# Later weight slices begin at stepped offsets inside longer buffers, in an attention and MLP kernel

## The chip, the cores and the metric

The kernel runs on one core of a Trainium2 chip. The metric is device time in microseconds (us) for one execution. A core has five engines that take part: TensorE (PE, with its weight loads shown apart as PEld), VectorE (DVE), ScalarE (ACT), GpSimd (POOL) and SyncE (SP), which issues transfers. Operands lie in an on-chip memory of 128 partitions; an address below is a byte offset within a partition.

## What is computed

Attention over 2 x 8 heads of 768 tokens with head size 64, masked so that a query sees only keys of its own hash bucket; then an MLP in two parts over the 1536 tokens. The weights named w1 to w4 in the kernel are those of the MLP.

```
scores = scale * np.matmul(q, k.transpose(0, 1, 3, 2))
scores = np.where(q_bucket[:, :, :, None] == k_bucket[:, :, None, :], scores, -1e9)
attn   = softmax(scores); x = attn @ v            # then heads side by side: [1536, 512]
h = np.maximum(np.maximum(x @ w1, x @ w2), x @ w3) # three matrices of 512 x 768
x = h @ w_out                                      # 768 x 512
h = x @ w_in                                       # 512 x 2048
g = np.where(h >= 1, h, np.where(h <= -1, 0.0, (h + 1) ** 2 / 4))
out = g @ w_out2                                   # 2048 x 512
```

## The kernel before

Every 32-bit operand of a large product is split into a high and a low part ("hi" and "lo", type fp32r), and a product is the sum of three matmuls: high x high, high x low, low x high (PARTS, line 264). `mm3` issues these (L271), and layer 4 has its own loop (L1012). Attention fills the first 208 us of the run, with the work of all engines put in order by a planner (class `Work`); neither the planner nor attention is touched by the change.

The MLP (function `mlp`) works through 58 slices of weights in a fixed list, `slices`: 18 of layer 1 (the three matrices that enter the maximum; 512 columns), 8 of layer 2 (384 columns), then 16 of layer 3 and 16 of layer 4 in alternation (512 columns). Tokens run in three chunks of 512. In layers 1 to 3 a slice is the stationary operand (128 x 128 blocks of it are loaded into TensorE) and the activations "x_hl" or "hh" stream past it. In layer 4 it is the other way round: the activations "g" are stationary and the slice is the moving operand, 512 columns at a time, the last token tile in two halves of 256.

A slice gets ready in steps (`w_steps`). A transfer brings the raw 64-bit numbers ("wr"); ScalarE and VectorE turn them into 32-bit numbers ("wg", "wg2", L205 to L222); ScalarE's copy at L228 writes the high part, `w[:, 0]`, and GpSimd's subtraction at L234 writes the low part, `w[:, 1]`, which starts 2,048 bytes behind the high part. The steps are interleaved with the matmuls by calls of `w_tick`. `w_done` frees a slice, and up to seven slices are ready or in the making at once. The first matmul that reads a slice waits for L234.

The seven buffers for split slices are of two kinds. Slice n goes to one of three buffers "w" if n % 7 < 3; these exist from the beginning of the run. Otherwise it goes to one of four buffers "wx", which are made when attention has ended and its memory is free. Each buffer is [128, 2, 512] of 4 bytes, 4,096 bytes in a partition. The wx buffers begin at byte 109,568, a multiple of 512, and follow one another; behind them lie "hh" and, after layer 2, in its place, "acc", "g" and "r". All of these begin at multiples of 512 bytes, as do w, x_hl and, for attention, "dt".

"dt" holds the transposed weights of attention; its last product (`block4`, L471) streams `dt[rows, at, kb]`, 6 runs of 32 numbers that start 128 bytes further for each key block kb, in groups of four matmuls (u_ps, t_ps twice, pj_ps) for each kb, even and odd kb behind one another.

Of the kernel before, what the change touches and what calls it, by code (L numbers as in the profile page):

```python
# [9 lines left out]
F32R = mybir.dt.float32r  # L10
# [103 lines left out]
def lsh_attention_moe_kernel(  # L114
# [60 lines left out]
    WEARLY, WBUFS = 3, 7  # L175
    raws, splits, low_todo = {}, {}, []
    w_state = {"raw": 0, "done": 0, "base": 0, "gen": None, "auto": False, "more": None}
# [10 lines left out]
    def w_load(upto):  # L188
        while w_state["raw"] < min(upto, NSL):
            n = w_state["raw"]  # L190
            _, src, cols = slices[n]
            r = w_p.tile([128, 512, 2], I32, tag="wr", name="wr", bufs=2)
            nc.sync.dma_start(out=r[:, 0:cols, :].rearrange("p c t -> p (c t)"), in_=src.bitcast(I32))
            raws[n] = r
            w_state["raw"] += 1

    def w_steps(n):
        w_load(n + 2)
        cols = slices[n][2]
        r = raws.pop(n)  # L200
        low, high = r[:, 0:cols, 0], r[:, 0:cols, 1]
        g = w_p.tile([128, 512], I32, tag="wg", name="wg", bufs=2)[:, 0:cols]
        if w_state["auto"]:
            w_low()
        nc.scalar.activation(out=f32(g), in_=f32(high), func=ACTF.Square)  # L205
        yield
        nc.vector.scalar_tensor_tensor(  # L207
            out=f32(g), in0=f32(g), scalar=TINY_SQ, in1=f32(high), op0=ALU.is_ge, op1=ALU.mult
        )
        yield  # L210
        g2 = w_p.tile([128, 512], I32, tag="wg2", name="wg2", bufs=2)[:, 0:cols]
        nc.vector.tensor_scalar(  # L212
            out=g2, in0=g, scalar1=3, scalar2=0x3FFFFFF8, op0=ALU.logical_shift_left, op1=ALU.bitwise_and
        )
        yield
        nc.vector.scalar_tensor_tensor(
            out=g2, in0=g, scalar=-0x40000000, in1=g2, op0=ALU.bitwise_and, op1=ALU.bitwise_or
        )
        yield
        nc.vector.scalar_tensor_tensor(  # L220
            out=g2, in0=low, scalar=29, in1=g2, op0=ALU.logical_shift_right, op1=ALU.bitwise_or
        )  # L222
        yield
        if n % WBUFS < WEARLY:
            w = w_p.tile([128, 2, 512], F32R, tag="w", name="w", bufs=WEARLY)
        else:
            w = w_state["more"].tile([128, 2, 512], F32R, tag="wx", name="wx", bufs=WBUFS - WEARLY)
        nc.scalar.copy(out=w[:, 0, 0:cols], in_=f32(g2))  # L228
        splits[n] = w
        low_todo.append((n, w, g2, cols))  # L230

    def w_low():
        for n, w, g2, cols in low_todo:
            nc.gpsimd.tensor_tensor(out=w[:, 1, 0:cols], in0=f32(g2), in1=f32(w[:, 0, 0:cols]), op=ALU.subtract)  # L234
        low_todo.clear()

    def w_tick(count=1):
        for _ in range(count):
            if w_state["gen"] is None:
                n = w_state["done"]  # L240
                if n >= NSL:
                    w_low()
                if n >= NSL or n >= w_state["base"] + (WBUFS if w_state["more"] else WEARLY):
                    return
                w_state["gen"] = w_steps(n)
            try:
                next(w_state["gen"])
            except StopIteration:
                w_state["gen"] = None
                w_state["done"] += 1  # L250
# [846 lines left out]
```

## Time and profile before

| | |
|---|---|
| runs, median (lowest to highest) | 668.21 us (667.55 to 668.88), 2 runs |
| span of the profiled execution, first to last instruction | 666.5 us |
| TensorE busy | 657.7 us, 99% |
| its weight loads | 527.7 us, 79% |
| VectorE, ScalarE, GpSimd busy | 485.4, 340.5, 275.7 us |
| mean granted clock of TensorE | 0.997 |

The profile is of one execution. A matmul's duration in it runs from its start to its modelled end, and matmuls overlap, so the time that each adds is read from the chain of work that ended last or from the distance between starts. Weight loads (PEld) overlap the matmul ahead of them.

### The profile page before, as it was taken

The page shows a single profiled execution, that of the slowest core. Times are in us where ns is not written, and L with a number is a line of the kernel's source. Part 1 is how long each engine was busy: PE and PEld are TensorE (multiplying, and loading weights), DVE is VectorE, ACT ScalarE, POOL GpSimd, SP SyncE. Part 2 cuts the span into 40 slices and gives each one's busy share as a digit, 9 for nine tenths or more (in the row PEclk, how much of TensorE's full clock was granted, in tenths as well). Part 3 has the DMA queues.
Part 4 walks back from the last instruction along what each step waited for, and adds up shares of the span by engine and source line. Part 5 has one row for each costly group of instructions (what it writes and reads, how often), then busy time and mean ns, then how long its engine had stood idle before and what let it go on. Part 6 is the DMA issues. An engine that isn't in the chain of part 4 may idle for free.

```text
span 666.5 us, 11515 instructions
## 1 busy us (share of the span) xinstructions
PE 657.7 (99%) x4413; PEld 527.7 (79%) x4413; DVE 485.4 (73%) x717; ACT 340.5 (51%) x632; POOL 275.7 (41%) x253
## 2 busy tenths in 40 slices
PE   7999999999999999999999999999999999999998
PEld 5667777777767888888888888888888888888886
DVE  5788989899763667875453466766888888888844
ACT  7687876887782233233222325665444444444430
POOL 6427547657322335344223113644444444444430
PEclk8999999999999999999999999999999999999999
DMA  6947786786243122322111122121121111211104
GB/s 188 227 121 183 203 213 175 190 235 172 86 133 82 64 95 74 116 74 62 47 49 56 55 73 87 40 74 53 63 64 64 63 65 63 64 63 64 32 0 189
DMA packets 27854, 66.97 MB, mean 100 GB/s; under 512 B 4164, under 2 KB 9124, under 8 KB 27800
## 3 DMA queue, kind: packets, MB, share of 16 engines
q1 hardware_dynamic: 27488, 66.21, 34.1%
q8 instruction: 34, 0.56, 0.4%
q14 instruction: 20, 0.16, 0.1%
q10 hardware_dynamic: 312, 0.04, 0.0%
HBM read 46.17 MB, written 3.19 MB: 74 GB/s over the span
## 4 chain that ended last, share of the span: by engine, by line
PE 97%; DMA 1%; ACT 0%; DVE 0%; POOL 0%; issue 0%; SPq 0%; ACTq 0%; DVEq 0%; POOLq 0%
PE b L271 49%; PE b L1012 20%; PE s_ps L410 6%; PE u_ps L504 5%; PE t_ps L443 5%; PE s_ps L413 5%; PE u_ps L471 3%; PE pj_ps L386 2%; PE t_ps L471 1%; DMA rb<-d 1%; DMA r<-in_kq 0%; PE pj_ps L471 0%; PE s_ps L271 0%; POOL q L377 0%; DVE p L420 0%; DMA d<-rt 0%
## 5 line engine op out<-in xcount | busy, mean ns | idle before, releaser
L271 PE MATMUL b<-x_hl,wx 128*128 128x512 f32 x684 | 159.6, 389 | 0.0
L271 PEld LDWEIGHTS b<-x_hl,wx 128*128 128x128 f32 x684 | 128.4, 188 | 26.7
L271 PE MATMUL b<-x_hl,w 128*128 128x512 f32 (+1 forms) x564 | 123.8, 376 | 0.0
L271 PEld LDWEIGHTS b<-x_hl,w 128*128 128x128 f32 x564 | 100.9, 188 | 19.8 <-issue 0.6
L912 POOL TENSOR_TENSOR g<-r,g 128x512 fp32r<-128x512 f32 x48 | 62.5, 1304 | 121.4 <-ACT g L911 121.4
L420 DVE TENSOR_SCALAR_CACHE_REDUCE p<-s_ps 128x768 f32<-128x768 f32 x96 | 89.7, 951 | 13.0 <-PE s_ps L413 9.6
L207 DVE SCALAR_TENSOR_TENSOR wg<-wg,wr 128x512 f32<-128x512 f32 (+1 forms) x58 | 67.2, 1159 | 37.6 <-ACT wg L205 36.9
L435 ACT ACTIVATE p<-p,nm 128x768 f32<-128x768 f32 x96 | 89.7, 936 | 6.4 <-DVE p L420 5.9
L410 PE MATMUL s_ps<-lo,q 128*128 128x384 f32 x192 | 72.4, 377 | 3.0 <-POOL lo L377 1.8
L234 POOL TENSOR_TENSOR wx<-wg,wx 128x512 fp32r<-128x512 f32 (+1 forms) x32 | 45.7, 1427 | 65.3 <-ACT wx L228 48.4
L1012 PE MATMUL b<-wx,g 128*128 128x512 f32 x288 | 72.1, 389 | 0.0
L1012 PE MATMUL b<-w,g 128*128 128x512 f32 (+1 forms) x294 | 71.4, 385 | 0.0
L228 ACT CAST wx<-wg 128x512 fp32r<-128x512 f32 (+1 forms) x32 | 19.3, 605 | 92.5 <-DVE wg L220 92.5
L413 PE MATMUL s_ps<-hi,q 76*128 76x384 f32 x192 | 65.8, 343 | 0.0
L992 DVE SCALAR_TENSOR_TENSOR r<-r,b 128x512 f32<-128x512 f32 x48 | 33.0, 687 | 44.3 <-ACT r L991 44.3
L1012 PEld LDWEIGHTS b<-w,g 128*128 128x128 f32 x294 | 54.5, 188 | 11.1
L1012 PEld LDWEIGHTS b<-wx,g 128*128 128x128 f32 x288 | 54.0, 188 | 11.2
L1019 DVE TENSOR_TENSOR acc<-b,acc 128x512 f32<-128x512 f32 (+1 forms) x85 | 56.3, 675 | 7.7 <-PE b L1012 7.6
L234 POOL TENSOR_TENSOR w<-wg,w 128x512 fp32r<-128x512 f32 (+1 forms) x26 | 36.0, 1384 | 48.5 <-ACT w L228 38.3
L212 DVE TENSOR_SCALAR wg<-wg 128x512 int32<-128x512 int32 (+1 forms) x58 | 53.6, 924 | 2.7
L990 ACT ACTIVATE r<-b,half_sb 128x512 f32<-128x512 f32 x48 | 33.0, 687 | 41.3 <-PE b L271 41.3
L410 PEld LDWEIGHTS s_ps<-lo,q 128*128 128x128 f32 x192 | 36.7, 191 | 21.5 <-DVE p L420 9.1
(92 smaller groups left out, 1042.2 us busy)
## 6 DMA issues: line engine op xcount, KB each, us to landing
wr<-in_w SPq DMA_DIRECT2D x48, 512.0 KB
r<-in_kq SPq DMA_DIRECT2D x15, 384.0 KB
q<-hi SPq DMA_DIRECT2D x15, 384.0 KB
v<-in_v SPq DMA_DIRECT2D x21, 256.0 KB
rb<-d SPq DMA_DIRECT2D x16, 192.0 KB
wr<-in_w SPq DMA_DIRECT2D x8, 384.0 KB
q<-lo SPq DMA_DIRECT2D x15, 192.0 KB
lo<-hi SPq DMA_DIRECT2D x15, 192.0 KB
```

What stands on the lines that cost most here:

```text
L207: nc.vector.scalar_tensor_tensor(out=f32(g), in0=f32(g), scalar=TINY_SQ, in1=f32(high), op0=ALU.is_ge, op1=ALU.mult)
L212: nc.vector.tensor_scalar(out=g2, in0=g, scalar1=3, scalar2=0x3FFFFFF8, op0=ALU.logical_shift_left, op1=ALU.bitwise_and)
L234: nc.gpsimd.tensor_tensor(out=w[:, 1, 0:cols], in0=f32(g2), in1=f32(w[:, 0, 0:cols]), op=ALU.subtract)
L271: nc.tensor.matmul(out=outp, lhsT=w_[a], rhs=x_[b_], start=(begins and i == 0 and jj == 0), stop=(ends and i == n - 1 and jj == 2),)
L410: nc.tensor.matmul(out=o, lhsT=hd["qa"][:, qs], rhs=hd["lo"][:, ks], start=True, stop=False)
L413: nc.tensor.matmul(out=o, lhsT=hd["qb"][0:76, qs], rhs=hd["hi"][0:76, ks], start=False, stop=True)
L420: nc.vector.tensor_scalar(out=p.rearrange("p (a k) -> p a k", a=2), in0=s_ps[bank.at][:, :, 0:HALF], scalar1=MASKED, scalar2=MASKED, op0=A ...
L435: nc.scalar.activation(out=p, in_=p, func=ACTF.Exp, scale=-1.0, bias=tl[n]["nm"], accum_out=sums_of(h // 2)[:, c:c + 1],)
L443: nc.tensor.transpose(out=t_ps[:, half, j * 128:(j + 1) * 128], in_=tl[n]["p"][:, kt * 128:(kt + 1) * 128], identity=ident,)
L912: nc.gpsimd.tensor_tensor(out=dst[:, 1, cs], in0=src, in1=f32(dst[:, 0, cs]), op=ALU.subtract)
L1012: nc.tensor.matmul(out=pb[:, cs], lhsT=gs[f][:, a, tsl], rhs=wt[:, b_, cs], start=(n == 0), stop=(n == len(terms) - 1),)
L1019: nc.vector.tensor_tensor(out=acc[:, t, cs], in0=pb[:, cs], in1=acc[:, t, cs], op=ALU.add)
```

## The change

The buffers wx become 1,152 numbers long, 4,608 bytes in place of 4,096. A slice takes 1,024 of these numbers in one piece, from a step on that counts the slices that went to wx before: 0 for the first, 4 numbers (16 bytes) for the second, and so on up to 124 numbers (496 bytes), and then from 0 again. `late` and `step` are worked out in Python while the program is built.

```diff
         if n % WBUFS < WEARLY:
             w = w_p.tile([128, 2, 512], F32R, tag="w", name="w", bufs=WEARLY)
         else:
-            w = w_state["more"].tile([128, 2, 512], F32R, tag="wx", name="wx", bufs=WBUFS - WEARLY)
+            late = sum(m % WBUFS >= WEARLY for m in range(n))
+            step = 4 * (late % 32)
+            w = w_state["more"].tile([128, 1152], F32R, tag="wx", name="wx", bufs=WBUFS - WEARLY)
+            w = w[:, step:step + 1024].rearrange("p (a c) -> p a c", a=2)
```

The program that is built has, on each engine, the same instructions in the same order, with the same semaphores waited for. The wx buffers begin at bytes 109,568, 114,176, 118,784 and 123,392, all multiples of 512, and hh, acc, g and r each begin 2,048 bytes later than before. The buffers w and all of attention stay where they were.

## Rows read from the trace of the kernel before

**Rows 1.** The page, part 1: busy us, share of the span, instructions.
```profile
span 666.5 us, 11515 instructions
...
PE 657.7 (99%) x4413; PEld 527.7 (79%) x4413; DVE 485.4 (73%) x717; ACT 340.5 (51%) x632; POOL 275.7 (41%) x253
```

**Rows 2.** The page, part 4: the chain that ended last, by engine.
```profile
PE 97%; DMA 1%; ACT 0%; DVE 0%; POOL 0%; issue 0%; SPq 0%; ACTq 0%; DVEq 0%; POOLq 0%
```

**Rows 3.** Busy time by stretch, from 219.0 to 663.2 us (x: instructions).
```profile
core 0: us, PE busy (x) PEld busy (x) DVE busy (x) ACT busy (x) POOL busy (x), PEclk, DMA share, GB/s
219.00:663.20 444.20, 444.20 (x1981) 368.59 (x1979) 312.11 (x398) 180.57 (x313) 164.06 (x121) 1.00 0.20 67
```

**Rows 4.** The chain in order of time: start us, us, engine, tile, line, matmuls.
```profile
451.19 2.72 PE b L271 x12
453.91 2.72 PE b L1012 x12
...
641.59 2.72 PE b L271 x12
644.31 19.12 PE b L1012 x90
```

**Rows 5.** Groups by shape, 219.0 to 663.2 us, TensorE: busy us, mean ns | idle before.
```profile
L271 PE MATMUL b<-x_hl,wx 128*128 128x512 f32 x684 | 159.6, 389 | 0.0
L271 PE MATMUL b<-x_hl,w 128*128 128x512 f32 x468 | 109.9, 389 | 0.0
L1012 PE MATMUL b<-wx,g 128*128 128x512 f32 x288 | 72.1, 389 | 0.0
L1012 PE MATMUL b<-w,g 128*128 128x512 f32 x282 | 70.0, 389 | 0.0
L271 PE MATMUL b<-hh,wx 128*128 128x512 f32 x135 | 31.2, 389 | 0.0
L271 PE MATMUL b<-hh,w 128*128 128x512 f32 x81 | 18.8, 389 | 0.0
...
L1012 PE MATMUL b<-w,g 128*128 128x256 f32 x12 | 1.6, 282 | 0.0
```

**Rows 6.** The same groups for the weight loads of the same stretch.
```profile
L271 PEld LDWEIGHTS b<-x_hl,wx 128*128 128x128 f32 x684 | 128.4, 188 | 26.7
```

**Rows 7.** Groups by shape over the span: the two writers of a split slice.
```profile
L234 POOL TENSOR_TENSOR wx<-wg,wx 128x512 fp32r<-128x512 f32 x27 | 40.3, 1491 | 39.0 <-ACT wx L228 28.2 <-issue 10.8
L234 POOL TENSOR_TENSOR w<-wg,w 128x512 fp32r<-128x512 f32 x23 | 32.9, 1431 | 40.0 <-ACT w L228 36.3 <-issue 3.8
L228 ACT CAST wx<-wg 128x512 fp32r<-128x512 f32 x27 | 16.8, 621 | 79.0 <-DVE wg L220 79.0
L228 ACT CAST w<-wg 128x512 fp32r<-128x512 f32 x23 | 14.3, 621 | 62.5 <-DVE wg L220 62.5
```

**Rows 8.** Tile wx, 223.0 to 231.5 and 540 to 553 us: ns min/median/max, starts.
```profile
L271 PEld LDWEIGHTS b<-x_hl,wx x5: 187/188/188, 230.5 to 231.4; 128*128 128x128 f32 x5
...
L234 POOL TENSOR_TENSOR wx<-wg,wx x2: 1298/1298/1299, 225.3 to 230.2; 128x512 fp32r<-128x512 f32 x2
...
L234 POOL TENSOR_TENSOR wx<-wg,wx x2: 1299/1520/1742, 539.4 to 545.6; 128x512 fp32r<-128x512 f32 x2
L228 ACT CAST wx<-wg x2: 620/622/625, 544.9 to 552.0; 128x512 fp32r<-128x512 f32 x2
```

**Rows 9.** Timeline of TensorE from 57.9 us: start us, us, instruction (L471).
```profile
57.80 0.32 PE L471 MATMUL u_ps<-dt,v 32*64 32x192 f32 x1
...
57.83 0.32 PE L471 MATMUL u_ps<-dt,v 32*64 32x192 f32 x1
...
57.96 0.32 PE L471 MATMUL u_ps<-dt,v 32*64 32x192 f32 x1
...
57.99 0.32 PE L471 MATMUL u_ps<-dt,v 32*64 32x192 f32 x1
...
58.12 0.32 PE L471 MATMUL u_ps<-dt,v 32*64 32x192 f32 x1
...
58.29 0.32 PE L471 MATMUL u_ps<-dt,v 32*64 32x192 f32 x1
```

## Prediction

> **What bounds the kernel now.** I read the page's list of engines first: TensorE (PE) is busy for 657.7 of 666.5 us, its weight loads 527.7 us, VectorE 485.4, ScalarE 340.5 and GpSimd 275.7 [rows 1]. The chain that ended last says the same from the other side: 97% of it is TensorE, 1% DMA, and VectorE, ScalarE and GpSimd round to nothing [rows 2]. Only work on TensorE, or a wait put in front of it, can move the end.
>
> The four buffers named "wx" exist only after attention, so the stretch that counts is what follows it. From 219.0 to 663.2 us, TensorE is busy for 444.20 of 444.20 us at a granted clock of 1.00, the higher of its two levels (2.4 GHz), while VectorE works 312 us of it, ScalarE 181 and GpSimd 164 [rows 3]. Nothing stalls it there: a wait that the change lengthens must first use up slack before it costs anything.
>
> What one matmul costs in that stretch is read from the chain, not from the durations. The listed 389 ns is latency: matmuls overlap. Twelve matmuls of 512 columns take 2.72 us, 226.7 ns each, in layer 1 to 3 (L271) and in layer 4 (L1012) alike [rows 4]. The last piece holds 90 matmuls in 19.12 us, and 12 of them are the 256-column ones [rows 4, 5]. So one of 256 columns costs (19.12 - 78 x 0.2267) / 12 = 0.120 us. Half the columns save 106.7 ns, or 0.417 ns a column, which is one column a cycle at 2.4 GHz. That leaves **13.3 ns a matmul that doesn't scale with columns**. This remainder is the only place where I see TensorE lose time, so it is what a change of addresses could remove, or double.
>
> **The change, part by part.** *Order and waits.* Each engine gets the same instructions in the same order with the same waits. No instruction is added: the sum of slices and the step are worked out when the program is built. So there is no count to cost; the whole question is whether an address changes what one instruction takes.
>
> *Where the slices lie.* 32 of the 58 slices go to wx, and there are 32 steps, so each offset from 0 to 496 bytes is used once. In order they are the 9 late slices of layer 1 (0 to 128), 5 of layer 2 (144 to 208) and 18 of layers 3 and 4 (224 to 496). The four buffers themselves still begin at multiples of 512 bytes. The matmuls that read them are 684 + 135, which take the slice as the stationary operand, and 288 of layer 4, which stream it as the moving operand: 1107 in all [rows 5]. Layer-4 matmuls hold "g" stationary, and that only moves by 2,048 bytes.
>
> *Weight loads.* A load of 128 x 128 takes 188 ns and hides behind the matmul ahead of it. Before the 684 loads from wx the load path sits idle for 26.7 us, 39 ns each [rows 6]. A load may thus lengthen by 39 ns, a fifth, at no cost. If that cover is gone, each ns beyond it costs 0.82 us over the 819 stationary reads.
>
> *Moving reads.* The 288 of layer 4 have no such cover. A read that took x ns longer would cost 0.288x us.
>
> *Writers.* ScalarE's copy into wx takes 621 ns, as into w; GpSimd's subtraction takes 1491 ns against 1431 [rows 7]. Both now write off the 512-byte grid. The tightest slice I see is the first one: GpSimd begins it at 225.3 us, takes 1.30, and TensorE begins to load it at 230.5 us, 3.9 us later. Late in the run a subtraction that begins at 545.6 us and takes at most 1.74 has 4.7 us until the copy into another buffer at 552.0, so GpSimd isn't crowded either [rows 8]. Twice the time for every subtraction would still be hidden in the first slice, and there is idle time for the rest (164 of 444 us busy). I cost the writers at 0.
>
> *Neighbours.* "hh", "acc", "g" and "r" begin 2,048 bytes later, still on the 512-byte grid. In the rows, matmuls on w and on wx, with x_hl, hh or g beside them, all cost the same 226.7 ns although these tiles lie far apart in many ways [rows 4, 5]. I cost this at 0.
>
> *Bounds of the unknown.* No row shows TensorE reading an operand that starts at an odd multiple of 16 bytes. The nearest is attention's last product (L471): its moving tile "dt" steps by 128 bytes from one key block to the next. Blocks come in pairs, and from pair to pair the start phase in 512 bytes turns between 0 with 128 and 256 with 384. The pairs start at 57.80, 57.96, 58.12 and 58.29 us: 0.16 or 0.17 us apart, whatever the phase [rows 9]. That row says 0 for steps of 128 bytes. For 16 bytes I bound it from both sides with the remainder: at best an off-grid read removes 13.3 ns, at worst it pays them again. Phase 0 takes 36 matmuls out, so 1071 x 13.3 = **14.3 us either way**. I take 0, nearest to rows 9.
>
> **The sum.** The profiled span of 666.5 us stays 666.5. The median of the runs shown is 668.21, so 1.7 us lie around the span, and the forecast for the measured time is **668.2 us**.
>
> **A page weighed.** The remainder was worked out above as 13.3 ns on each 512-column matmul [rows 4, 5]. The Trainium skill ("TensorE: Matmul & The Clock Gate", section "Back-to-back issue gap") gives N/2.4 + 2.5 ns between isolated warm matmuls, 215.8 ns for 512 columns, measured there on bf16. By that figure 10.9 ns of the 226.7 would be avoidable, and if equal address phases were the cause, the estimate from the page would be 1071 x 10.9 = 11.7 us less. The same page's step-by-step description says that TensorE has two independent read ports, one for the streamed operand and one for weight loads; that speaks against any collision between the two. No run here shows yet which holds.
>
> **The rivals.** *Faster: the remainder is a collision of equal phases.* In the kernel before, weights and streamed operand both start on the 512-byte grid, in every matmul of the MLP. If that costs the 13.3 ns, 1071 matmuls lose it and the time is 668.2 - 14.3 = **653.9 us**. For it: the remainder is there in every matmul, and no row varies the phase of one operand against the other by less than 128 bytes. Against it: it is the same to the nanosecond for 512 and 256 columns, in all layers, and with the slice stationary or moving, and rows 9 show no phase effect. A collision that arises only for part of the phases would give less, about 661.
>
> *Slower: an off-grid start costs a second remainder.* If a slice that begins off the grid makes TensorE fetch its rows in one more piece, each such matmul pays 13.3 ns again: 668.2 + 14.3 = **682.5 us**. It decides (more than 2%, 13.4 us) from 12.5 ns a matmul on. For it: nothing in the trace excludes it below 128 bytes. Against it: for the 819 stationary reads the longer fetch would have to exceed the 39 ns of cover first. So a milder form is likelier: only the 288 moving reads pay, 3.8 us, **672.0 us**.
>
> *The change doesn't do what it says* is excluded: the buffers begin on the grid and each step occurs once.
>
> **How the numbers follow.** No change at 668.2: 88%, with a range of its own from 666.5 to 670, which is the spread of the two runs (667.55 to 668.88) and 1 us for another chip or a small tail. Moving reads alone pay, 672.0: 4%. All off-grid reads pay, 682.5: 3%. Part of the remainder goes, about 661: 2%. All of it goes, 653.9: 3%. The range of 666.0 to 671.5 leaves both far ends out and reaches most of the way to the mild case. Faster or slower means by over 2%, about what a measurement of this kernel can tell from no change: faster 0.03 (653.9), slower 0.03 (682.5), within 2% the other 0.94.
>
> **What would show it.** If I am right, the chain after 219 us still has pieces of 12 matmuls in 2.72 us on every slice, and loads from wx still take 188 ns. If the fast rival holds, pieces on wx take 2.56 us beside 2.72 on w, in one and the same profile; if the slow one, 2.88. If only moving reads pay, L1012 on wx departs and L271 doesn't. If the writers were wrong, the subtraction into wx lengthens against that into w, and a wait of TensorE for it appears. My forecast is wrong if wx and w differ at all in ns per matmul.

## The result, and the profile after

The changed kernel took 676.9 us (median of 2 runs, 676.48 to 677.32) against 668.21: a ratio of 1.0131 with a 95% interval of 1.0101 to 1.0160. A second comparison on another occasion, with more runs, gave 1.0087 (1.0063 to 1.0111), 5.8 us by the ratio. So the change makes the kernel slower by about 1%. The forecast was 668.2 with a range of 666.0 to 671.5; it was too low, and its range missed the time.

The page, part 1, of the changed kernel, answers to [rows 1]:

```profile
span 674.7 us, 11515 instructions
...
PE 666.1 (99%) x4413; PEld 528.9 (78%) x4413; DVE 486.4 (72%) x717; ACT 340.5 (50%) x632; POOL 275.4 (41%) x253
```

The span grew by 8.2 us, and TensorE's busy time by 8.4. The other engines' busy times moved by 1 us at most. Busy time by stretch, for the MLP from 221.0 us (the same columns as in [rows 3]):

```profile
221.00:671.20 450.20, 450.20 (x1980) 368.65 (x1979) 311.72 (x398) 180.63 (x313) 164.15 (x121) 1.00 0.20 66
```

TensorE still never waits there, and its granted clock is still 1.00. So neither a wait nor the clock explains the loss there: the same matmuls take longer. Which ones, the groups by shape of that stretch show beside [rows 5] (lines are 3 further down, L271 is now L274, L1012 is L1015):

```profile
L274 PE MATMUL b<-x_hl,wx 128*128 128x512 f32 x684 | 162.6, 393 | 0.0
L274 PE MATMUL b<-x_hl,w 128*128 128x512 f32 x468 | 110.3, 390 | 0.0
L1015 PE MATMUL b<-wx,g 128*128 128x512 f32 x288 | 73.7, 394 | 0.0
L1015 PE MATMUL b<-w,g 128*128 128x512 f32 x282 | 70.3, 390 | 0.0
L274 PE MATMUL b<-hh,wx 128*128 128x512 f32 x135 | 31.9, 394 | 0.0
L274 PE MATMUL b<-hh,w 128*128 128x512 f32 x81 | 18.9, 390 | 0.0
```

In matmuls on wx the sums rise by 3.0 us in layers 1 and 3, 1.6 in layer 4 and 0.7 in layer 2: 4.4, 5.6 and 5.2 ns a matmul. Matmuls on w, which nobody moved, rise by 0.4, 0.3 and 0.1. Together that is **6.1 us**.

The other 2.0 us of the span lie ahead of the MLP. Its first pieces in the chain start at 210.37 us in the changed kernel and at 208.34 in the kernel before. Two of the experiments below, both without any loss in the MLP, have it at 207.74 and 210.11. One fence for each kernel (before; changed; long buffers only; steps of 256 bytes):

```profile
208.34 31.83 PE b L271 x173
```
```profile
210.37 29.79 PE b L274 x164
```
```profile
207.74 32.28 PE b L274 x175
```
```profile
210.11 30.02 PE b L274 x165
```

Attention's length thus varies by up to 2.4 us between executions of identical attention code, and the change's own part is the 6.1 us of the MLP, which fits the second comparison's 5.8 us.

What happened inside one slice is seen by cutting the chain to it. Here are 35 matmuls each from the first slice on wx (offset 0), the third (32 bytes) and the fifth (64 bytes), then 29 from the slice at 240 bytes, and pieces of 12 from layers 3 (L274) and 4 (L1015), the last four late in the run:

```profile
232.91 7.93 PE b L274 x35
...
249.24 8.16 PE b L274 x35
...
290.53 8.17 PE b L274 x35
...
416.48 6.57 PE b L274 x29
...
450.48 2.72 PE b L274 x12
...
641.29 2.80 PE b L1015 x12
644.09 2.74 PE b L274 x12
646.83 2.80 PE b L1015 x12
649.63 2.74 PE b L274 x12
```

Offset 0 keeps 226.6 ns a matmul, 32 bytes cost 233.1, 64 bytes 233.4. The piece at 450.48 is mostly in the slice at 256 bytes, and it keeps 2.72 us. The slices at 240 and 496 bytes, 16 short of a multiple of 256, come out clean too: behind slower ones the first three matmuls take longer, and the rest 226.6 (the 29 from 416.48 on; the two pieces of 2.74 us are the slice at 496). The chain also shows what w pays for. Here is the slice on w that follows the one at 48 bytes:

```profile
265.80 2.07 PE b L274 x9
...
267.86 5.67 PE b L274 x25
```

Its first nine matmuls take 230.0 ns each, the next 25 are back at 226.8. The loads answer to [rows 6]; they still take 188 ns, and only the idle time ahead of them grew:

```profile
L274 PEld LDWEIGHTS b<-x_hl,wx 128*128 128x128 f32 x684 | 128.6, 188 | 29.5
```

The writers, too, are as in [rows 7]: 1490 ns for the subtraction into wx, 621 for the copy.

```profile
L237 POOL TENSOR_TENSOR wx<-wg,wx 128x512 fp32r<-128x512 f32 x27 | 40.2, 1490 | 39.1 <-ACT wx L231 28.2 <-issue 10.9
...
L231 ACT CAST wx<-wg 128x512 fp32r<-128x512 f32 x27 | 16.8, 621 | 78.7 <-DVE wg L220 78.7
```

### The profile page after: what moved, and what is told of

Its sections match the earlier page's. It is cut to its first block, busy times and chain, and to the rows that moved or that the text cites. A ratio compares the mean times of both kernels' runs of the same rounds, so it can differ in the third digit from the quotient of the medians.

```text
span 674.7 us, 11515 instructions
## 1 busy us (share of the span) xinstructions
PE 666.1 (99%) x4413; PEld 528.9 (78%) x4413; DVE 486.4 (72%) x717; ACT 340.5 (50%) x632; POOL 275.4 (41%) x253
## 4 chain that ended last, share of the span: by engine, by line
PE 97%; ACT 1%; POOL 0%; DMA 0%; DVE 0%; issue 0%; DVEq 0%; ACTq 0%; POOLq 0%
PE b L274 49%; PE b L1015 20%; PE s_ps L413 6%; PE t_ps L446 6%; PE u_ps L507 5%; PE s_ps L416 5%; PE u_ps L474 3%; PE pj_ps L389 2%; PE t_ps L474 1%; PE pj_ps L474 0%; DMA r<-in_kq 0%; PE s_ps L274 0%; ACT pt L456 0%; POOL q L380 0%; DVE pt L456 0%
## 5 line engine op out<-in xcount | busy, mean ns | idle before, releaser
L274 PE MATMUL b<-x_hl,wx 128*128 128x512 f32 x684 | 162.6, 393 | 0.0
L274 PEld LDWEIGHTS b<-x_hl,wx 128*128 128x128 f32 x684 | 128.6, 188 | 29.5
L274 PE MATMUL b<-x_hl,w 128*128 128x512 f32 (+1 forms) x564 | 124.2, 376 | 0.0
L274 PEld LDWEIGHTS b<-x_hl,w 128*128 128x128 f32 x564 | 100.9, 188 | 20.4 <-issue 0.6
L1015 PE MATMUL b<-wx,g 128*128 128x512 f32 x288 | 73.7, 394 | 0.0
L1015 PE MATMUL b<-w,g 128*128 128x512 f32 (+1 forms) x294 | 71.7, 386 | 0.0
L1015 PEld LDWEIGHTS b<-wx,g 128*128 128x128 f32 x288 | 54.0, 188 | 12.6
L1015 PEld LDWEIGHTS b<-w,g 128*128 128x128 f32 x294 | 54.5, 188 | 11.5
```

What stands on the lines that cost most here:

```text
L274: nc.tensor.matmul(out=outp, lhsT=w_[a], rhs=x_[b_], start=(begins and i == 0 and jj == 0), stop=(ends and i == n - 1 and jj == 2),)
L1015: nc.tensor.matmul(out=pb[:, cs], lhsT=gs[f][:, a, tsl], rhs=wt[:, b_, cs], start=(n == 0), stop=(n == len(terms) - 1),)
```

## The experiments

Phase means here the remainder of an operand's address by 256 bytes, and distance the difference of two phases. The theory formed from these rows (A): what counts is the phase of the weights that TensorE loads against the phase of the operand that streams. Rivals: the moved neighbours or the longer buffers (B), the change of offset from slice to slice (C), the absolute address (A-absolute). "MLP cost" below is worked out as above, from the busy sums of the six groups against those of the kernel before, here over the whole span, where x_hl against w counts 492 matmuls and 115.7 us before.

| kernel | ratio to the kernel before (95%) | MLP cost |
|---|---|---|
| change, second time | 1.0087 (1.0063 to 1.0111) | 6.1 us |
| long buffers, offset 0 | 1.0000 (0.9981 to 1.0019) | 0 |
| offsets 0 and 256 | 1.0006 (0.9987 to 1.0024) | 0 |
| offset 128 for all of wx | 1.0113 (1.0087 to 1.0140) | 7.4 us |
| everything up by 128 | 1.0011 (0.9993 to 1.0028) | 0 |
| only x_hl apart by 128 | 1.0115 (1.0085 to 1.0145) | 8.0 us |
| low parts up by 128 | 1.0132 (1.0104 to 1.0160) | 8.4 us |
| own operands apart, by turns | 1.0047 (1.0024 to 1.0071) | 3.8 us |
| load apart from stream, by turns | 1.0055 (1.0033 to 1.0077) | 4.0 us |
| offset 16 for all of wx | 1.0047 (1.0024 to 1.0069) | 2.8 us |
| steps on layer 4 only | one run, 672.45 beside 669.45 us | 2.7 us |
| steps of 4 bytes | one run, 674.26 beside 669.28 us | 7.1 us |

**The change once more.**

> The changed kernel once more, beside the kernel before on one chip. By the traces its MLP stretch is 6.1 us longer than before, and the 2.0 us more ahead of it lie in attention, which is the same code and began its MLP between 207.7 and 210.0 us in kernels that leave it alone. If only the MLP part is the change's, the medians differ by 6 to 7 us (ratio 1.009 to 1.010); if attention really is slower too, by 8 to 9 us (1.013).

Ratio 1.0087, 5.8 us, and the same sums by group as the first profile. The MLP part is the change's; the extra 2 us of the first comparison fit attention's spread.

**Long buffers only.** One line of the change is undone:

```diff
-            step = 4 * (late % 32)
+            step = 0
```

> The buffers stay 4,608 bytes long, but every slice begins at byte 0 of its buffer; hh, acc, g and r lie 2,048 bytes later, as in the change. Theory A (the phase of a slice within 512 bytes costs TensorE time): matmuls on wx are back at 226.7 ns, 668 us. Theory B (the longer buffers and the moved neighbours cost the time): about 676 us, wx at 231 to 232 ns as in the change.

```profile
L274 PE MATMUL b<-x_hl,wx 128*128 128x512 f32 x684 | 159.6, 389 | 0.0
```

No difference, and every group is within 0.1 us of its old sum. Theory B falls: the longer buffers and neighbours 2,048 bytes further cost nothing.

**Offsets of 0 and 256 bytes.**

```diff
-            step = 4 * (late % 32)
+            step = 64 * (late % 2)
```

> Slices begin at 0 and 256 bytes by turns. In the profile of the change the one slice at 256 cost 226.7 ns a matmul, as the one at 0 did, and most others 230 to 234. Theory A1 (phases count within 256 bytes): 226.7 ns on all slices, 668 us. Theory A2 (phases count within 512 bytes, and the slice at 256 was clean by chance): 16 of the 32 slices pay 5 to 6 ns on some 550 matmuls, about 3 us more, 671 us.

```profile
L274 PE MATMUL b<-x_hl,wx 128*128 128x512 f32 x684 | 159.6, 389 | 0.0
...
L1015 PE MATMUL b<-wx,g 128*128 128x512 f32 x288 | 72.1, 389 | 0.0
```

The groups by shape stand at their old sums: the grid is one of 256 bytes (A1), not 512.

**Offset 128 for all.**

```diff
-            step = 4 * (late % 32)
+            step = 32
```

> All late slices begin at byte 128 of their buffer. Theory A (an offset against the 256-byte grid costs): each of the 1107 matmuls on wx pays about 5 to 6 ns, 5.5 to 6.6 us more plus under 1 us on w, so 674 to 675 us. Theory C (it is the change of offset from slice to slice, or the multiples of 16 that are no multiples of 64, that cost): 226.7 ns, 668 us.

```profile
L274 PE MATMUL b<-x_hl,wx 128*128 128x512 f32 x684 | 163.6, 395 | 0.0
...
L1015 PE MATMUL b<-wx,g 128*128 128x512 f32 x288 | 73.7, 394 | 0.0
```

4.0 us over 684 matmuls are 5.8 ns each, 1.6 over 288 again 5.6. The stepping isn't needed (C falls); a constant 128 bytes costs more than the mixture, of which some slices were clean.

**Everything up by 128.** The kernel before, with an unused 128-byte tile at the front of memory:

```diff
+    shift = const.tile([128, 32], F32, name="shift")
+    nc.vector.memset(shift, 0.0)
     pj_raw = const.tile([128, 64], F32, name="pj_raw")
```

> The kernel before with an unused tile of 128 bytes ahead of everything: all tiles of attention and of the MLP begin at 128 instead of 0 within 256 bytes, so every weight slice and the operand that streams beside it (or is held beside it) keep the same phase to each other. Theory A-relative (what counts is the phase of the loaded weights against the streamed operand): 226.7 ns everywhere, 668 us. Theory A-absolute (any read that begins off the grid is slower): all 1938 matmuls of 512 columns pay 5 to 6 ns, 678 to 680 us.

```profile
L273 PE MATMUL b<-x_hl,wx 128*128 128x512 f32 x684 | 159.6, 389 | 0.0
L273 PE MATMUL b<-x_hl,w 128*128 128x512 f32 x492 | 115.7, 389 | 0.0
L1014 PE MATMUL b<-wx,g 128*128 128x512 f32 x288 | 72.1, 389 | 0.0
```

No cost at all, though every operand begins off the 256-byte grid. The absolute address doesn't count here; the relation between operands does.

**Only x_hl apart.** The tile is put behind x_hl in place of ahead of it, so weights, hh and g move together and x_hl stays:

```diff
     x_hl = x_p.tile([128, 2, 4, NT], F32R, name="x_hl")
+    shift = x_p.tile([128, 32], F32, name="shift")
+    nc.vector.memset(shift, 0.0)
```

> The kernel before with an unused tile of 128 bytes behind x_hl: all weight buffers, hh, g and attention's tiles begin at 128 within 256 bytes, x_hl stays at 0. No slice moves against its buffer. Theory A-relative: every matmul of layers 1 and 3 (x_hl against w or wx, 1176 of 512 columns) takes 231 to 233 ns, layer 2 (hh against weights, both at 128) stays at 226.7, layer 4 (g against weights, both at 128) pays only for the first few matmuls behind a layer-3 group; 6 to 7.5 us more, 675 to 676 us. Theory W (only an offset of the weights within wx counts): 226.7 ns, 668 to 669 us.

```profile
L273 PE MATMUL b<-x_hl,wx 128*128 128x512 f32 x684 | 163.9, 395 | 0.0
L273 PE MATMUL b<-x_hl,w 128*128 128x512 f32 x492 | 118.7, 395 | 0.0
L1014 PE MATMUL b<-wx,g 128*128 128x512 f32 x288 | 72.5, 390 | 0.0
L1014 PE MATMUL b<-w,g 128*128 128x512 f32 x282 | 70.2, 390 | 0.0
L273 PE MATMUL b<-hh,wx 128*128 128x512 f32 x135 | 31.3, 389 | 0.0
```

Every matmul with x_hl pays 6.1 to 6.3 ns, on w as on wx; layer 2 pays nothing to speak of, layer 4 about 1 ns, at its turns with layer 3. The weights' own buffers have nothing to do with it.

**Which relation?** In the trace of the kernel before, each weight load starts 3 to 4 ns behind the start of a matmul, the one ahead of its own. So two pairs could matter: a load and the stream that runs at the same time (L), or a matmul's own weights and stream (M). First the low parts were put 128 bytes apart from the high ones, by longer tiles, as here:

```diff
-            w = w_p.tile([128, 2, 512], F32R, tag="w", name="w", bufs=WEARLY)
+            w = w_p.tile([128, 2, 544], F32R, tag="w", name="w", bufs=WEARLY)
```

> In x_hl, w, wx, hh and g the low part begins 128 bytes further, within 256 bytes, than the high part. The three matmuls of a product load high, high, low and stream high, low, high. So in two of three the weights stand at another phase than the operand that streams past them, but each load (which starts as the matmul ahead of its own starts) meets a streaming operand of its own phase: high weights load beside a high stream, low weights beside a low one. Theory L (a load and the stream that runs at the same time must have one phase): 226.7 ns everywhere, 668 to 669 us. Theory M (a matmul's own two operands must have one phase): two thirds of 1962 matmuls pay 5 to 8 ns, 6.5 to 10 us more, 675 to 679 us.

```profile
L271 PE MATMUL b<-x_hl,wx 128*128 128x512 f32 x684 | 162.6, 393 | 0.0
L271 PE MATMUL b<-x_hl,w 128*128 128x512 f32 x492 | 117.8, 393 | 0.0
L1012 PE MATMUL b<-wx,g 128*128 128x512 f32 x288 | 73.3, 393 | 0.0
```

Some 4.2 to 4.4 ns on all matmuls: L alone falls, and M's two thirds of 5 to 8 ns fit. (Here, too, two of three streams begin at another phase than the stream ahead of them, so S, below, fits as well.) But two cleaner kernels, in which layers 1 and 3 alternate between two row blocks, don't leave M alone either. In both, the order of the matmuls is

```diff
-        for i, (w_, x_) in enumerate(pairs):
-            for jj, (a, b_) in enumerate(PARTS):
...
+            for two in (pairs[:2], pairs[2:]):
+                line += [(w_[a], x_[b_]) for a, b_ in PARTS for w_, x_ in two]
```

and odd row blocks of x_hl and of the slices are laid out 128 bytes off the grid; in the first of the two, all of x_hl stands another 128 bytes on.

> Layers 1 and 3 take their four blocks of 128 rows two at a time and alternate between them (high x high of both, then high x low, then low x high), with x_hl and the slices laid out so that the phase within 256 bytes turns between 0 and 128 with every matmul: each matmul's own two operands are 128 bytes apart, while each load has the phase of the operand that streams while it runs (that of the matmul ahead). Layers 2 and 4 keep one phase. Theory L (load against the stream of the same time): layers 1 and 3 at 226.7 ns, 668 to 670 us. Theory M (a matmul's own two operands): some 231 to 235 ns on 1178 matmuls of 512 columns, 5 to 9 us more, 674 to 678 us. Theory S (what costs is that successive streams change their phase): also slow, here and in the next kernel.

> The same alternation, but with both operands of a matmul at one phase, 0 and 128 by turns: each load is 128 bytes apart from the operand that streams while it runs. Theory L: layers 1 and 3 at 231 to 235 ns, 674 to 678 us. Theory M: 226.7 ns, 668 to 670 us. Theory S: slow as in the kernel with the own operands apart.

The groups of the first, then of the second:

```profile
L295 PE MATMUL b<-x_hl,wx 128*128 128x512 f32 x684 | 161.9, 392 | 0.0
L295 PE MATMUL b<-x_hl,w 128*128 128x512 f32 x492 | 117.2, 392 | 0.0
L1037 PE MATMUL b<-wx,g 128*128 128x512 f32 x288 | 72.1, 389 | 0.0
...
L295 PE MATMUL b<-x_hl,w 128*128 128x256 f32 x72 | 9.3, 281 | 0.0
```
```profile
L291 PE MATMUL b<-x_hl,wx 128*128 128x512 f32 x684 | 161.1, 391 | 0.0
L291 PE MATMUL b<-x_hl,w 128*128 128x512 f32 x492 | 116.6, 391 | 0.0
L1033 PE MATMUL b<-wx,g 128*128 128x512 f32 x288 | 73.0, 392 | 0.0
```

Own operands apart: 2.3 us over 684, 3.4 ns each. Load apart from the running stream: 1.5 us, 2.2 ns each. Neither L nor M returned to 226.7; the first pays a good half, the second over a third of the 5.8 to 6.3 ns of a constant distance. The second also pays 0.9 us in layer 4 on wx (73.0 against 72.1), and 0.6 on w (70.6 against 70.0), though layer 4 keeps one phase there: its groups follow those of layer 3. In both kernels successive streams also alternate (S). S can't be the whole cause, since with a constant 128 bytes all streams have one phase and pay most. No run has the new order of the matmuls with all operands at one phase, so a share of the order itself isn't excluded either. Whether the two relations add, or the alternation or the order has a share, stays open.

**Layer 4 only.**

```diff
-            step = 4 * (late % 32)
+            step = 4 * (late % 32) if slices[n][0][0] == "4" else 0
```

> The change with its steps on the slices of layer 4 alone (8 of the 32), which stream while g is loaded; all others begin at byte 0. If the phase of load against stream counts whichever of the two is moved, layer 4 keeps its 231 to 233 ns on 288 matmuls (1.6 us) and layers 1 and 2 return to 226.7, layer 3 to within 1 ns of it, about 2 us over before in all. If only weights that are loaded off the grid cost, all is at 226.7.

```profile
L274 PE MATMUL b<-x_hl,wx 128*128 128x512 f32 x684 | 160.0, 390 | 0.0
L274 PE MATMUL b<-x_hl,w 128*128 128x512 f32 x492 | 116.1, 390 | 0.0
L1015 PE MATMUL b<-wx,g 128*128 128x512 f32 x288 | 73.7, 394 | 0.0
```

Layer 4 keeps its 1.6 us, with the streaming operand moved and the loaded one in place; layer 2 is clean (31.2 us on wx). So a distance costs whichever side moves. Layer 3 pays 0.4 us on wx and as much on w though none of its operands moved: the loss is carried over from the layer-4 group ahead of it. The total came to 2.7 us; 2 were expected.

**Steps of 4 bytes, and 16 for all.**

```diff
-            step = 4 * (late % 32)
+            step = late % 32
```

> As in the change, but with steps of 4 bytes: the slices begin at 0, 4, 8 ... 124. The profile of the change had 226.7 to 226.9 ns at 0, 16 and 256, and 230 to 234 from 32 on. Theory A says that a short distance is free, so slices up to some 16 bytes (the first five) take 226.7 ns and later ones 230 to 234, and none less than 226.7. If what counts is whole steps of 16 bytes and nothing finer, the offsets 4, 8, 12 would cost what 0 or 16 do; if odd starts cost by themselves, 4 to 12 cost more than 16 does.

The slice at 4 bytes, then the one at 16:

```profile
237.88 7.90 PE b L274 x34
...
287.11 7.93 PE b L274 x35
```

232.4 ns at 4 bytes and 226.6 at 16: a small distance isn't free, only 16 of those below 32 was (8, 12, 20, 24 and 28 bytes took 230.0 to 234.9 by the starts in the same trace). None went below 226.6. The slice at 16 stands behind three on w, at distance 0, and not straight behind the one at 12, as the next expectation has it. Whether 16 is free by itself was then tried in all slices:

```diff
-            step = 4 * (late % 32)
+            step = 4
```

> All late slices begin at byte 16 of their buffer. In the profile of the change the slice at 16 cost 226.7 to 226.9 ns a matmul, and with steps of 4 bytes again 226.7, straight behind a slice at 12 that cost 230. If 16 bytes of distance are free, all 1107 matmuls on wx stay at 226.7 to 227 ns and the time is that of the kernel before, 668 to 670 us. If the two slices were clean only because the rhythm of a grid slice ahead was carried on, slices behind others, above all the turns of layers 3 and 4, pay up to 6 ns, up to 674 us.

The chain of that kernel, where layer 4 first reads slices of wx:

```profile
450.73 2.72 PE b L274 x12
453.45 2.77 PE b L1015 x12
456.23 2.79 PE b L274 x12
459.01 2.78 PE b L1015 x12
461.79 2.74 PE b L274 x12
```

All of layers 1 and 2 (offset 16, read behind a clean slice) stayed at 226.7. When layer 4 streams its slices with that distance the other way round, 2.77 us appear, and at 456.23 layer 3, which was clean at 450.73 with the same distance, is slow too. At 16 bytes a clean rhythm is kept, but a lost one comes back only at times: of 17 groups of layer 3 at that distance behind a slow group, 12 stay slow throughout (2.79 or 2.80 us) and 5 recover on the way (2.74, as at 461.79). At distance 0 it comes back within about ten matmuls. That is also why unmoved slices on w paid 0.8 us in the change. The distance alone isn't the whole rule: from weights to stream, layer 3 on the slice at 240 bytes in the change has the same one within 256 bytes as layer 4 has here, and it returned to 226.6, where layer 4 turns slow behind a clean group. Why the two differ stays open.

## Why the prediction was wrong

*What bounds the kernel* held. TensorE alone decides, no wait and no writer came into play, loads stayed at a mean of 188 ns, the neighbours were free, and the clock was the same. That much of the forecast of "no change" was right, and it is why the whole loss is one of ns per matmul.

*The step that failed is the bound of the unknown*: "I take 0, nearest to rows 9". Rows 9 show matmuls of 192 columns with 32 rows and 64 weight columns, four of them at a time; they show no effect of 128 bytes. At 128 x 128 with 512 columns the same 128 bytes cost 5.8 ns. The row was near in its steps of address, but not in what it streams and loads, and I took its zero as the centre and 88% of the chance. Nor could its pairs show the effect: each holds one block at 0 or 256 and one at 128 or 384, so within 256 bytes, the period that the runs show, all pairs are alike, and equal spacing from pair to pair says nothing about 128 bytes. With the upper bound kept in the range, it would have reached 682.5 us and held the 676.9.

*The rival "slower" named the sign and not the size.* It priced 13.3 ns on 1071 matmuls, 14.3 us; measured were 4.4 to 5.6 ns on 1107 and 0.8 us on w, 6.1 us. It also tied the cost to a read that begins off the grid, which moving everything by 128 bytes refutes. *"Only moving reads pay"* is wrong too: 3.7 of the 6.1 us were paid by matmuls that load the moved slices. The reason against a cost for stationary reads, 39 ns of cover, looked at the wrong quantity: the loads' mean stayed at 188 ns, their cover grew, and the matmuls drew apart all the same.

*The rival "faster"* took the remainder of 13.3 ns for a collision of equal phases. It is the reverse: equal phases are the best found, and every distance tried was slower or, 16 bytes from the grid on either side, at best equal. The Trainium skill ("TensorE: Matmul & The Clock Gate", section "Back-to-back issue gap") gives 215.8 ns between isolated warm matmuls of 512 columns; no stretch on 512 columns here came near it, 226.6 ns was the least. The same page of the Trainium skill states two independent read ports (section "Step-by-step: what each phase is for"). No run here shows the ports themselves, but taken as "phases can't matter" the statement misled: they do, by 2 to 6 ns a matmul.

*The list of what would show it* served: "if wx and w differ at all in ns per matmul" is what the first look at the groups showed.

## What to carry to other kernels

In a kernel like this one, which TensorE bounds without a wait, the addresses of its operands are part of its speed: keep loaded weights and streamed operand at one phase within 256 bytes, for all tiles that meet in a chain of matmuls. Padding a tile by 128 bytes, or one odd tile between two pools, can cost 1% here, and shifting all of them together by 128 bytes cost nothing. And a row that bounds an unknown cost must be alike in size and form of the operands, and must be able to show the effect; being near in the one thing that is changed is not enough. Where there is no such row, the far bound belongs in the range.

## What the runs showed of the hardware that was not expected

- The distance between stationary and moving operand counts within 256 bytes: 0 and 256 cost 226.7 ns a matmul of 512 columns, a constant 128 costs 232.5 (on wx) to 233.0 (on all of x_hl), 4 bytes 232.4, 32 bytes 233.1.
- There is a memory from one matmul to the next. A slice of layers 1 to 3 at 16 bytes stays at 226.7 ns behind a clean one, and behind a disturbed one it stayed slow in 12 groups of 17; distance 0 recovers within about ten matmuls. The cause inside TensorE isn't shown by any row.
- Matmuls of 256 columns go the other way: 72 of them take 9.3 us in place of 9.5 in both kernels whose phases alternate by 128 bytes, some 3 ns less each. There are too few here to use it.
